# Softmax in 64-column chunks: the subtraction and the sum move from VectorE to ScalarE

## The chip, the cores and the metric

One core of a Trainium2 chip runs the whole program. The metric is the device time of one execution in microseconds (us), here 1665.19 us as the median of 3 runs before the change (1658.57 to 1665.71). Engines are named as in the profile: PE is TensorE (matmul) and PEld its weight load, DVE is VectorE, ACT is ScalarE, POOL is GpSimd, SP is SyncE, which only issues DMAs here.

## The reference

Attention within chunks of 64 tokens feeds two gated products. The change concerns the first function alone.

```python
def _attn_ref(q, k, v):                      # 8 batches, 8 heads, 576 tokens, 64 per head
    q_c, k_c, v_c = ...                      # 9 chunks of 64 tokens each
    scores = scale * np.matmul(q_c, k_c.transpose(0, 1, 2, 4, 3))
    scores = scores - np.max(scores, axis=-1, keepdims=True)
    attn = np.exp(scores)
    attn = attn / (np.sum(attn, axis=-1, keepdims=True) + 1e-09)
    out = np.matmul(attn, v_c)

x = _attn_ref(q, k, v)                       # as 4608 tokens x 512
x = (x @ w_a) * (x @ w_b) @ w_out            # inner width 1536
h = ((x @ w1) * (x @ w2)) @ w3               # inner width 1024
return h @ w_out2
```

## The kernel before, in words

The 4608 tokens are nine blocks of 512. A unit (class `Unit`) is one block and one pair of heads, so there are 36 units. Its scores are 16 products of 64x64: chunk n of the block goes to bank i = n mod 2 of two PSUM banks `s[0]` and `s[1]`, and the two heads stand on the upper and the lower 64 partitions. So each of the two banks holds four chunks of 64 columns (`chunks`, 256 of the bank's 512 columns), and the tile `e` in SBUF (128x512) holds all eight, sorted by `by_parity`.

The steps of a unit are: `load1`, `load2` (q, k, v by DMA), `turn` (q and k transposed: by VectorE, or in the first four blocks by TensorE with a copy by ScalarE out of two banks), `scores`, `soft1` (maximum per chunk and partition, subtraction, exponential), `soft2` (sum, plus 1e-9, reciprocal, multiplication), `flip` and `flip2` (`e` transposed into `pT`, by VectorE, or in the first four blocks by TensorE into a bank and a copy by ScalarE), `apply` (times v) and `put` (two copies of 128x256 out of PSUM, L410).

Nothing reorders the program at run time: each engine works through its own queue in the order in which the code emits, and waits there on semaphores. Four units stand alone in a prologue (the loop at L1174). The pieces of all others are emitted at the calls of `point()` between the products of the two gated layers. Blocks 0 and 1 are multiplied plainly (`plain_step`, L950); the later blocks go in pairs through a Strassen scheme with seven products per step (`strassen_step`, L895). Its order is P5, P1, P2, P6, P3, P7, P4 on the banks C, A, B, A, C, A, A: P6 and P4 add onto what P1 and P7 left in bank A, after ScalarE or VectorE has read the intermediate state (`held` is a copy c22, c11 or c12 by ScalarE, L914; `add` is VectorE's, L917). Behind P7 come the second layer's matmuls `acc` (L858) of the step before. L829 is the matmul line of all seven products and L815 that of the plain ones.

Units that run inside this loop use the PSUM banks that `state["banks"]` names: ("rB", "rD"). rB is also the bank of P2. Inside a burst of second-layer matmuls (`burst`, L985) they are acc2 and acc3. There is one buffer for each of the tiles `mx`, `sm`, `e` and `pT` outside of the prologue.

ScalarE also rounds every operand's high part (`split`, L242), converts weights (L180) and copies the plain products (L959). VectorE also forms low parts (L243), converts weights (L179 to L189) and multiplies.

Of the kernel before, what the change touches and what calls it, by code (L numbers as in the profile page):

```python
# [9 lines left out]
F32 = mybir.dt.float32  # L10
# [3 lines left out]
AF = mybir.ActivationFunctionType  # L14
ALU = mybir.AluOpType
AX = mybir.AxisListType

P = 128
NT = 512
CH = 64  # L20
# [58 lines left out]
def chunk_attention_two_gated_products(  # L79
# [23 lines left out]
    nc = tc.nc  # L103
# [8 lines left out]
    NCH = NT // CH  # L112
    HALF = NT // 2
    scale = 1.0 / float(D) ** 0.5
# [3 lines left out]
    pool = ctx.enter_context(tc.tile_pool(name="pool", bufs=1))  # L118
# [135 lines left out]
    class Unit:  # L254
# [93 lines left out]

        def soft1(self):
            mx = pool.tile([P, 2, NCH // 2], F32, tag="mx", name=f"mx{self.nm}")  # L350
            self.e = self.work("e")
            e4 = self.by_parity(self.e)
            for i in range(2):
                nc.vector.tensor_reduce(mx[:, i], self.chunks(self.s[i]), axis=AX.X, op=ALU.max)
            for i in range(2):
                nc.vector.tensor_tensor(
                    e4[:, i],
                    self.chunks(self.s[i]),
                    mx[:, i].unsqueeze(2).to_broadcast([P, NCH // 2, CH]),
                    op=ALU.subtract,  # L360
                )
            nc.scalar.activation(self.e, self.e, AF.Exp, scale=scale)

        def soft2(self):
            sm = pool.tile([P, NCH], F32, tag="sm", name=f"sm{self.nm}")
            e3 = self.e.rearrange("p (n k) -> p n k", k=CH)
            nc.vector.tensor_reduce(sm, e3, axis=AX.X, op=ALU.add)
            nc.vector.tensor_scalar_add(sm, sm, 1e-9)
            nc.vector.reciprocal(sm, sm)
            nc.vector.tensor_tensor(  # L370
                e3, e3, sm.unsqueeze(2).to_broadcast([P, NCH, CH]), op=ALU.mult
            )
# [720 lines left out]
    with tc.manual_schedule():  # L1093
# [241 lines left out]
        for ph, sb in [(0, sb) for sb in range(1, NSB + 1)] + [(1, sb) for sb in range(NSB + 1)]:  # L1335
# [39 lines left out]
            if lone:  # L1375
# [16 lines left out]
                class After:  # L1392
                    n = 0
# [71 lines left out]
```

## Time and profile before

| | |
|---|---|
| runs | 1665.71, 1665.19, 1658.57 us |
| profiled execution | span 1664.4 us from first to last instruction (the page gives no other time for it), mean granted TensorE clock 0.983 |
| PE busy | 1570.5 us, 94% |
| DVE busy | 899.0 us, 54% |
| ACT busy | 551.0 us, 33% |
| POOL busy | 571.5 us, 34% |
| chain that ended last | PE 73%, DVE 8%, DMA 5%, issue 4%, SP's queue 3%, ACT 3%, POOL 3% |

Busy times are sums over an engine's instructions. The chain is followed back from the last instruction, at each step to what released it. The busy share is an average over stages: attention lies in the first 880 us, where VectorE and ScalarE are fuller than behind. In a timeline an instruction stands with its start and duration in us; in brackets is the idle time of its engine before it and what ended that. In the granted clock, 1.00 is 2.4 GHz and 0.50 is 1.2 GHz.

### The profile page before, as it was taken

Reading aid. Unit: us, or ns where it says so; the run is one execution under the profiler, and the core shown is the slowest. Engines: PE = TensorE matmul, PEld = TensorE weight load, DVE = VectorE, ACT = ScalarE, POOL = GpSimd, SP = SyncE. Lnnn points to the kernel's source line nnn. Section 1 sums busy time; section 2 is a strip of 40 time slices with the busy share of each in tenths; the row PEclk is TensorE's granted clock in tenths of the full one; section 3 lists DMA queues with packets and bytes.
Section 4 is the critical chain, followed back from the end, with each engine's and each line's share of the span. In section 5 each row is a group of like instructions: output and inputs, shape, how many; then the busy total and the mean of one; then the engine's idle time right before and its main releaser. Section 6 shows DMA issues by size and latency. Waiting matters only on the chain.

```text
span 1664.4 us, 24572 instructions
## 1 busy us (share of the span) xinstructions
PE 1570.5 (94%) x8968; PEld 1256.9 (76%) x8968; DVE 899.0 (54%) x1460; ACT 551.0 (33%) x989; POOL 571.5 (34%) x578
## 2 busy tenths in 40 slices
PE   4789999899999999898999899999999999999998
PEld 3568777777776777676787677788878878878887
DVE  5768864786756555546776345554452352342331
ACT  4444534332342222332234222333332231331322
POOL 1435553322243211433446323323432332331432
PEclk9789999999999999999999999999999999999999
DMA  8668766887777777688997888886776666666684
GB/s 222 206 199 264 246 212 207 249 251 226 246 217 209 203 224 230 196 236 287 303 310 248 285 278 323 314 309 231 253 243 215 210 237 212 222 227 201 220 290 160
DMA packets 289976, 400.38 MB, mean 241 GB/s; under 512 B 175680, under 2 KB 196160, under 8 KB 289856
## 3 DMA queue, kind: packets, MB, share of 16 engines
q1 hardware_dynamic: 262688, 309.67, 60.9%
q0 software_dynamic: 23616, 81.80, 12.7%
q10 hardware_dynamic: 3552, 7.34, 1.2%
q8 instruction: 71, 1.16, 0.3%
q14 instruction: 49, 0.40, 0.1%
HBM read 312.74 MB, written 85.98 MB: 240 GB/s over the span
## 4 chain that ended last, share of the span: by engine, by line
PE 73%; DVE 8%; DMA 5%; issue 4%; SPq 3%; ACT 3%; POOL 3%; POOLq 0%; DVEq 0%; ACTq 0%
PE P L829 39%; PE acc L858 20%; PE wf L1082 3%; PE pb L815 3%; PE pa L815 3%; SPq L148 3%; DMA wo<-dwo 2%; PE pa0L L815 2%; PE pb0L L815 1%; PE x L396 1%; DVE c L917 1%; PE s L345 1%; ACT xP L242 1%; DMA d<-cv 1%; POOL cv L195 1%
## 5 line engine op out<-in xcount | busy, mean ns | idle before, releaser
L829 PE MATMUL P<-xP,w 128*128 128x512 f32 (+1 forms) x3102 | 715.5, 383 | 20.2 <-DVE c L917 16.5
L829 PEld LDWEIGHTS P<-xP,w 128*128 128x128 f32 x3102 | 557.0, 188 | 148.0 <-DVE c L917 23.3
L917 DVE TENSOR_TENSOR c<-P,c 128x512 f32<-128x512 f32 (+1 forms) x228 | 150.2, 661 | 302.5 <-PE P L829 301.8
L914 ACT COPY c<-P 128x512 f32<-128x512 f32 (+1 forms) x228 | 128.4, 563 | 222.9 <-PE P L829 222.3
L945 POOL TENSOR_TENSOR G<-c,c 128x512 f32<-128x512 f32 x68 | 88.6, 1304 | 311.1 <-DVE c L917 310.9
L242 ACT CAST gh<-c 128x512 fp32r<-128x512 f32 x68 | 42.3, 621 | 346.5 <-DVE c L944 346.5
L243 POOL TENSOR_TENSOR gl<-c,gh 128x512 fp32r<-128x512 f32 x68 | 90.3, 1328 | 162.3 <-ACT gh L242 158.7
L858 PE MATMUL acc<-gh,wo 128*128 128x512 f32 x384 | 138.8, 400 | 0.0
L944 DVE TENSOR_TENSOR c<-P,c 128x512 f32<-128x512 f32 x68 | 47.0, 691 | 137.7 <-PE P L829 137.7
L858 PE MATMUL acc<-wo,gh 128*128 128x512 f32 x320 | 111.2, 390 | 0.5 <-ACT gh L242 0.5
L858 PEld LDWEIGHTS acc<-gh,wo 128*128 128x128 f32 x384 | 72.8, 190 | 16.6
L195 POOL TENSOR_TENSOR cv<-cv 128x512 f32<-128x512 f32 x40 | 46.9, 1172 | 101.7 <-DVE cv L189 101.6
L243 DVE TENSOR_TENSOR xP<-xP,xP 128x512 fp32r<-128x512 f32 (+1 forms) x56 | 63.9, 1182 | 25.9 <-ACT xP L242 25.9
L815 PE MATMUL pa<-xq,w 128*128 128x512 f32 x288 | 76.0, 416 | 0.0
L858 PE MATMUL acc<-gl,wo 128*128 128x512 f32 x192 | 75.7, 394 | 0.0
L815 PE MATMUL pb<-xq,w 128*128 128x512 f32 x288 | 74.3, 409 | 0.0
L858 PEld LDWEIGHTS acc<-wo,gh 128*128 128x128 f32 x320 | 60.1, 188 | 13.9 <-ACT gh L242 1.0
L815 PEld LDWEIGHTS pa<-xq,w 128*128 128x128 f32 x288 | 57.1, 201 | 13.2
L867 ACT COPY ev<-acc 128x512 f32<-128x512 f32 x72 | 42.3, 587 | 71.0 <-PE acc L858 65.9
L815 PEld LDWEIGHTS pb<-xq,w 128*128 128x128 f32 x288 | 55.1, 196 | 11.6
L858 PE MATMUL acc<-wo,gl 128*128 128x512 f32 x160 | 63.0, 394 | 0.8 <-POOL gl L243 0.8
L157 POOL DMA_DIRECT2D dw<-w x58 | 32.4, 559 | 83.2 <-DVE w L243 80.3
(160 smaller groups left out, 2458.6 us busy)
## 6 DMA issues: line engine op xcount, KB each, us to landing
w<-dw SPq DMA_DIRECT2D x213, 512.0 KB, 4.4
wo<-dwo SPq DMA_DIRECT2D x168, 512.0 KB, 4.8
dw<-w POOLq DMA_DIRECT2D x58, 512.0 KB, 4.8
w<-dw SPq DMA_DIRECT2D x87, 256.0 KB, 3.3
d<-cv POOLq DMA_DIRECT2D x40, 256.0 KB, 5.2
su<-d SPq DMA_DIRECT2D x20, 512.0 KB, 4.9
cv_o<-in_moe_w_out_dram SPq DMA_DIRECT2D x18, 512.0 KB, 5.7
x2d<-ev POOLq DMA_DIRECT2D x36, 256.0 KB, 5.1
```

The source lines that it names most:

```text
L148: nc.sync.dma_start(*asks["left"].popleft())
L195: eng.tensor_tensor(self.w, hi.bitcast(F32), lo, op=ALU.add)
L242: nc.scalar.copy(dst_h, src)
L243: eng_l.tensor_tensor(dst_l, src, dst_h, op=ALU.subtract)
L815: nc.tensor.matmul(ps, w[m][:, kk // 2, wp, kk % 2], xq[kk // 2][:, kk % 2, xp], start=(n == 0), stop=(n == 3 * KM - 1),)
L829: nc.tensor.matmul(ps, w[:, wp, kt], x[:, kt, xp], start=(begins and n == 0), stop=(n == 5), skip_group_check=True,)
L858: nc.tensor.matmul(acc[m], a, b, start=(f == 0 and (wp, gp) == SEQ[0]), stop=(f == NF[ph] - 1 and (wp, gp) == SEQ[-1]),)
L914: nc.scalar.copy(t, src)
L917: add = lambda o, a, b: nc.vector.tensor_tensor(o, a, b, op=ALU.add)
L944: nc.vector.tensor_tensor(g, last, c11, op=ALU.mult)
L945: nc.gpsimd.tensor_tensor(g_place(ph, nm.split("_")[0], f, gplaces), c22, c12, op=ALU.mult)
L1082: nc.tensor.matmul(ps, t[:, gp, jj], wo2[jj // 2][:, jj % 2, wp], start=(jj == 0 and (wp, gp) == SEQ[0]), stop=(jj == NF[1] - 1 and (wp, g ...
```

## The change

The maxima are stored negated and multiplied by the scale in one more small VectorE instruction. VectorE's two subtractions and the single exponential over `e` are replaced by eight exponentials on ScalarE, one for each chunk of 64 columns, read straight out of the two score banks in alternation, each with the chunk's column of `mx` as its bias. Each of them also gives its chunk's sum into a column of `sm`, so the sum in `soft2` is gone. `sm` is now taken in `soft1`.

```diff
         def soft1(self):
             mx = pool.tile([P, 2, NCH // 2], F32, tag="mx", name=f"mx{self.nm}")
+            self.sm = pool.tile([P, NCH], F32, tag="sm", name=f"sm{self.nm}")
             self.e = self.work("e")
-            e4 = self.by_parity(self.e)
             for i in range(2):
-                nc.vector.tensor_reduce(mx[:, i], self.chunks(self.s[i]), axis=AX.X, op=ALU.max)
-            for i in range(2):
-                nc.vector.tensor_tensor(
-                    e4[:, i],
-                    self.chunks(self.s[i]),
-                    mx[:, i].unsqueeze(2).to_broadcast([P, NCH // 2, CH]),
-                    op=ALU.subtract,
+                nc.vector.tensor_reduce(
+                    mx[:, i], self.chunks(self.s[i]), axis=AX.X, op=ALU.max, negate=True
                 )
-            nc.scalar.activation(self.e, self.e, AF.Exp, scale=scale)
+            nc.vector.tensor_scalar_mul(mx, mx, scale)
+            for n in range(NCH):
+                m, i = divmod(n, 2)
+                nc.scalar.activation(
+                    self.e[:, n * CH : n * CH + CH],
+                    self.s[i][:, m * CH : m * CH + CH],
+                    AF.Exp,
+                    bias=mx[:, i, m : m + 1],
+                    scale=scale,
+                    accum_out=self.sm[:, n : n + 1],
+                )
 
         def soft2(self):
-            sm = pool.tile([P, NCH], F32, tag="sm", name=f"sm{self.nm}")
+            sm = self.sm
             e3 = self.e.rearrange("p (n k) -> p n k", k=CH)
-            nc.vector.tensor_reduce(sm, e3, axis=AX.X, op=ALU.add)
             nc.vector.tensor_scalar_add(sm, sm, 1e-9)
```

Lines behind the change stand four lines further down in the changed kernel (L829 becomes L833).

ScalarE's queue around the second unit of the third block pair, between P5 and P1. `c_1` are copies out of the products' banks (the first is c22, the second c11), `gh` and `w` are roundings, `s_4_1` are the two score banks of this unit. Before:

```order
L242 CAST gh_0_3543<-c_0_3455 128x512
L914 COPY c_1_3561<-P_1_3551 128x512
L362 ACTIVATE e_1_3586<-e_1_3586 128x512
L914 COPY c_1_3606<-P_1_3596 128x512
L242 CAST w_2_1_3621<-su_2_3433 128x2x256
L914 COPY c_1_3638<-P_1_3596 128x512
```

And now (the eight exponentials alternate between the two banks):

```order
L242 CAST gh_0_3628<-c_0_3540 128x512
L918 COPY c_1_3646<-P_1_3636 128x512
L360 ACTIVATE e_1_3672,sm_1_3671<-s_4_1_3652,mx_1_3670 128x64
L360 ACTIVATE e_1_3672,sm_1_3671<-s_4_1_3653,mx_1_3670 128x64
...
L918 COPY c_1_3698<-P_1_3688 128x512
L242 CAST w_2_1_3713<-su_2_3518 128x2x256
L918 COPY c_1_3728<-P_1_3688 128x512
```

What was one instruction out of SBUF between the copies of c22 and c11 is now eight out of PSUM, at the same place.

TensorE's queue at that place, with the semaphores that an instruction waits for (Activation is ScalarE's): the last scores, P1 and P2. Before:

```order
L345 MATMUL s_4_1_3568<-kT_1_3345,qT_1_3344 64x64 x2
L829 MATMUL P_1_3596<-xP_3110,w_1_0_3001 128x512 [waits DVE_49]
L829 MATMUL P_1_3596<-xP_3110,w_1_0_3001 128x512 x5
L829 MATMUL P_1_3608<-xP_3137,w_1_0_3001 128x512 [waits DVE_49,PE_49]
L829 MATMUL P_1_3608<-xP_3137,w_1_0_3001 128x512 x5
```

And now:

```order
L345 MATMUL s_4_1_3653<-kT_1_3432,qT_1_3431 64x64 x2
L833 MATMUL P_1_3688<-xP_3190,w_1_0_3081 128x512 [waits DVE_49]
L833 MATMUL P_1_3688<-xP_3190,w_1_0_3081 128x512 x5
L833 MATMUL P_1_3700<-xP_3217,w_1_0_3081 128x512 [waits DVE_49,Activation_49]
L833 MATMUL P_1_3700<-xP_3217,w_1_0_3081 128x512 x5
```

P2, the fourth and fifth row, now waits for ScalarE, since the last reader of the score bank in rB is an exponential.

VectorE's queue at the fourth unit of the third pair's second block, where `soft2` follows `soft1` at once; the last row is the addition that empties P7's bank. Before:

```order
L354 TENSOR_REDUCE mx_3_4966<-s_5_3_4948 128x4
L354 TENSOR_REDUCE mx_3_4966<-s_5_3_4949 128x4
L356 TENSOR_TENSOR e_3_4967<-s_5_3_4948,mx_3_4966 128x4x64
L356 TENSOR_TENSOR e_3_4967<-s_5_3_4949,mx_3_4966 128x4x64
L367 TENSOR_REDUCE sm_3_4973<-e_3_4967 128x8
L368 TENSOR_SCALAR sm_3_4973<-sm_3_4973 128x8
L369 RECIPROCAL sm_3_4973<-sm_3_4973 128x8
L370 TENSOR_TENSOR e_3_4967<-e_3_4967,sm_3_4973 128x512
L917 TENSOR_TENSOR c_10_4876<-P_10_4884,c_10_4876 128x512
```

And now:

```order
L354 TENSOR_REDUCE mx_3_5081<-s_5_3_5063 128x4
L354 TENSOR_REDUCE mx_3_5081<-s_5_3_5064 128x4
L357 TENSOR_SCALAR mx_3_5081<-mx_3_5081 128x8
L372 TENSOR_SCALAR sm_3_5082<-sm_3_5082 128x8
L373 RECIPROCAL sm_3_5082<-sm_3_5082 128x8
L374 TENSOR_TENSOR e_3_5083<-e_3_5083,sm_3_5082 128x512
L921 TENSOR_TENSOR c_10_4991<-P_10_4999,c_10_4991 128x512
```

Three long instructions are gone and a short one has come; L372 now is what waits for ScalarE, and the rest of the queue stands behind it as it stood behind L367.

## Rows read from the trace of the kernel before

**Rows 1.** The page's busy times: us, share of the span, instructions.
```profile
PE 1570.5 (94%) x8968; PEld 1256.9 (76%) x8968; DVE 899.0 (54%) x1460; ACT 551.0 (33%) x989; POOL 571.5 (34%) x578
```

**Rows 2.** Busy times in a stretch, by engine; last: clock, DMA share, GB/s.
```profile
42.00:200.00 158.00, 140.93 (x1096) 110.22 (x1095) 119.85 (x205) 73.19 (x123) 74.64 (x83) 0.92 0.73 228
```

**Rows 3.** Whom TensorE waited for, whole span: us in total, times, longest.
```profile
PE P L829 <- DVE c L917: 16.5, 15, 4.2
PE f L480 <- DVE e L370: 16.3, 9, 4.6
```

**Rows 4.** Instruction groups by form: busy us, mean ns, idle before and its releasers.
```profile
L914 ACT COPY c<-P 128x512 f32<-128x512 f32 x204 | 119.4, 586 | 210.3 <-PE P L829 209.9
...
L356 DVE TENSOR_TENSOR e<-s,mx 128x256 f32<-128x256 f32 x72 | 26.9, 415 | 0.0
...
L367 DVE TENSOR_REDUCE sm<-e 128x8 f32<-128x512 f32 x36 | 24.3, 674 | 3.8 <-ACT e L362 3.8
...
L362 ACT ACTIVATE e<-e 128x512 f32<-128x512 f32 x36 | 22.8, 633 | 96.3 <-DVE e L356 96.3
...
L410 ACT COPY x<-x 128x256 f32<-128x256 f32 x56 | 18.1, 376 | 24.5 <-PE x L396 24.1
```

**Rows 5.** Timeline of ScalarE, 326 to 329 us: start, duration, what, how many.
```profile
327.08 0.65 ACT L410 COPY x<-x 128x256 f32<-128x256 f32 x2 [2.41 <-PE x L396]
```

**Rows 6.** Timeline of one softmax after P3, 465 to 473 us.
```profile
465.83 0.74 DVE L354 TENSOR_REDUCE mx<-s 128x4 f32<-128x256 f32 x2
...
466.50 0.75 DVE L356 TENSOR_TENSOR e<-s,mx 128x256 f32<-128x256 f32 x2
...
467.34 0.63 ACT L362 ACTIVATE e<-e 128x512 f32<-128x512 f32 x1 [2.69 <-DVE e L356]
...
468.00 0.69 DVE L367 TENSOR_REDUCE sm<-e 128x8 f32<-128x512 f32 x1 [0.76 <-ACT e L362]
...
468.72 0.17 DVE L368 TENSOR_SCALAR sm<-sm 128x8 f32<-128x8 f32 x1
...
469.17 0.69 DVE L370 TENSOR_TENSOR e<-e,sm 128x512 f32<-128x512 f32 x1
...
470.51 1.66 PE L829 MATMUL P<-xP,w 128*128 128x512 f32 x6 [1.10 <-DVE c L917]
```

**Rows 7.** Timeline of one softmax between P5 and P1, 333 to 337 us.
```profile
333.01 1.66 PE L829 MATMUL P<-xP,w 128*128 128x512 f32 x6
334.18 0.74 DVE L354 TENSOR_REDUCE mx<-s 128x4 f32<-128x256 f32 x2
...
335.40 1.94 PE L829 MATMUL P<-xP,w 128*128 128x512 f32 x7 [0.72 <-DVE e L356]
```

**Rows 8.** Timeline of TensorE, 380 to 388 us: P4.
```profile
385.79 1.67 PE L829 MATMUL P<-xP,w 128*128 128x512 f32 x6 [1.77 <-DVE c L917]
```

**Rows 9.** Timeline of TensorE in the prologue: the fourth flip.
```profile
38.61 1.09 PE L480 MATMUL f<-ident,e 128*128 128x128 f32 x4 [4.56 <-DVE e L370]
```

**Rows 10.** Timeline of the first unit after the prologue, 50 to 58 us.
```profile
50.56 0.76 DVE L354 TENSOR_REDUCE mx<-s 128x4 f32<-128x256 f32 x2 [0.20 <-PE s L345]
...
52.61 1.04 ACT L468 COPY qT<-t 128x512 f32<-128x512 f32 x1
53.44 1.12 ACT L468 COPY kT<-t 128x512 f32<-128x512 f32 x1
...
54.73 0.90 PE L480 MATMUL f<-ident,e 128*128 128x128 f32 x4 [1.92 <-DVE e L370]
```

**Rows 11.** Timeline of TensorE, 118 to 126 us: a flip after a backlog.
```profile
123.64 0.63 PE L480 MATMUL f<-ident,e 128*128 128x128 f32 x4 [1.10 <-DVE e L370]
```

**Rows 12.** Timeline of TensorE, 224 to 236 us, after a wait for a DMA.
```profile
224.45 0.63 PE L467 MATMUL t<-ident,qk 128*128 128x128 f32 x4 [2.52 <-DMA qk<-in_k_dram]
224.83 4.58 PE L815 MATMUL pb<-xq,w 128*128 128x512 f32 x12
```

**Rows 13.** Busy times in the stretch behind it; the third number from the end is the clock.
```profile
225.00:230.00 5.00, 5.00 (x17) 3.92 (x16) 0.55 (x1) 1.52 (x2) 2.85 (x4) 0.66 0.39 117
```

## The prediction

> **What bounds the kernel now.** I read the page's table of busy times first, then the busy times by stretch, then who TensorE waited for, then the timelines around single softmaxes. TensorE is busy for 1570.5 of the 1664.4 us [rows 1], so the time changes only where an edit opens or closes a gap on TensorE. VectorE and ScalarE have idle time on average, and work taken from one or given to the other is by itself worth nothing. All 36 softmaxes lie in the first 880 us. There VectorE is crowded in one stretch, 119.85 of 158 us between 42 and 200 us [rows 2], and TensorE's two largest waits in the whole span are for VectorE: 16.5 us for the additions that empty a product's bank, and 16.3 us for the normalised `e` that the flip transposes [rows 3]. So softmax does stand on the path in places: this change is decided by how long one softmax takes from its scores to its `e`, by when it gives back its two PSUM banks, and by what is queued behind it on ScalarE.
>
> **What goes and what comes, per unit.** VectorE loses two subtractions of 415 ns and one sum of 674 ns [rows 4], and gains one small multiplication, priced below at 0.20 us: 1.3 us less per unit, 47 us in all. ScalarE loses one 633 ns exponential [rows 4] and gets eight of 128x64 out of PSUM, each with a bias read per partition and a sum to write out. No row shows that form. The nearest is the copy of 128x256 out of PSUM, 376 ns [rows 4]. Call E the time from the first of the eight to the end of the last.
>
> - Low end: the copies of 128x512 and 128x256 take 586 and 376 ns [rows 4], so 0.82 ns a column and 218 ns for 64 columns. Two of 128x256 in a row end 0.65 us after the first began [rows 5], so the second adds 0.27 us and a run overlaps by about 0.1. Eight then take 7 x 0.115 + 0.218 = 1.0 us, if bias and sum are free.
> - High end: each as long as the whole exponential of today, 633 ns: E = 5.1 us.
> - I take the nearest row unshortened, 376 ns each: E = 3.0 us. The smaller size pulls it down; the bias, and a sum that has to be delivered eight times, pull it up. Over 36 units ScalarE then gets 36 x (3.0 - 0.63) = 85 us more, which its average load would bear.
>
> **Break-even of a softmax.** In the unit at 465.83 us the maximum ends at 466.57, the exponential runs from 467.34, the sum starts at 468.00 and the normalisation ends at 469.86 [rows 6]. Afterwards: 466.57, plus 0.20 for the multiplication (the addition of the same size at 468.72 takes 0.17, and some 0.03 pass behind it), 0.09 to ScalarE (the subtraction ends at 467.25, today's exponential starts at 467.34), E, 0.03 back, and 1.14 for the small addition, the reciprocal and the normalisation (the 1.86 from sum to end, less the sum's own 0.72): 468.03 + E. The chain gets shorter only if E is under 1.83 us. With 3.0 it is 1.17 us longer.
>
> **Where that reaches TensorE.** Units whose softmax has slack (more than half of them) cost nothing: their flip comes several products later, and that work is the cover. The others, by place:
>
> 1. Five units after P5 (the second or third of a block pair, in L895's step): their scores stand between P5 and P1, and use the banks rB and rD. P2 writes into rB next and so must wait until the scores are read. Today the subtraction frees them: in the first, P1 starts at 333.01 and P2 at 335.40, 0.72 late [rows 7]. After the change the seventh of the eight exponentials frees that bank: maximum's end + 0.29 + 7/8 E. With 334.92 as that end, P2 starts at 337.84, 2.44 us later. The other four, with P1's 1.38 us as cover today, come out the same way at 2.74, 2.41, 2.41 and 2.40. Sum 12.4 us. The copy of c11, queued behind the eight on ScalarE, would end at about 338.8 and still hide beside P2, whose six matmuls take as long as P1's (1.66 us [rows 7]). VectorE's relief does not help here, since the bank's last reader has moved to ScalarE.
> 2. Two units after P3, where soft2 follows soft1 at once on VectorE and the addition that empties P7's bank stands behind it: P4 waits 1.10 us at 470.51 [rows 6]. The addition moves with the chain: 2 x 1.17 = 2.3 us. Two more of this kind have the transposes of q and k in between (P4's wait of 1.77 at 385.79 [rows 8]); there 2.7 us of E are covered, 0.3 each: 0.6 us.
> 3. The prologue: four units, each flip waiting for its `e`, the fourth for 4.56 us [rows 9], with ScalarE's casts for the weight conversion queued behind the exponentials and VectorE's conversion waiting for these casts. Three at the price of the tight chain; the fourth has slack, since VectorE converts in between, and gets half: 3.5 x 1.17 = 4.1 us.
> 4. Two units of the next block (the flips at 54.73 and 99.67): the maximum starts at 50.56, and the two copies of qT and kT, 1.95 us together, stand behind the exponential on ScalarE. The flip takes the bank that kT's copy empties, so it goes at 51.32 + 0.29 + E + 1.95 + 0.05 = 56.61 instead of 54.73 [rows 10]. 1.9 us each: 3.75 us.
> 5. Two units where VectorE comes to the sum late, out of a backlog, with the exponential long done: the flip's wait of 1.10 at 123.64 [rows 11] and its like at 188.78. Here the dropped sum is a gain, 0.7 us each: -1.4 us.
> 6. The clock. After a wait of 2.52 us at 224.45 the granted clock is 0.66 in 225 to 230 us, the level of 1.2 GHz for most of it, and twelve matmuls take 4.58 us [rows 12, 13]; after the wait of 1.77 at 385.79 six took 1.67, as many as at 333.01 behind no such wait [rows 7, 8]. Twelve at that pace would be 3.1 us, with the last one's tail of 0.2 counted once. The five waits of place 1 would be 2.4 to 3.2 us long, so each might cost another 1.5 us. The wait at 224.45 lay in a thinly filled stretch, these lie between full products; I take half: 3.8 us.
>
> Sum: 12.4 + 2.3 + 0.6 + 4.1 + 3.75 - 1.4 + 3.8 = 25.5 us on the span of 1664.4, so 1689.9. The page gives no other time for the profiled execution; its span is 0.8 us under the median of the runs (1665.2), which are themselves 7 us apart. Forecast: 1690 us.
>
> **Rivals.**
> - *The exponentials overlap.* If each of the eight adds what the second copy of the pair adds [rows 5], E = 0.376 + 7 x 0.27 = 2.27. Then place 1 is 9.2, place 2 is 0.9, the prologue 1.5, place 4 is 2.3, place 5 still -1.4, the clock nothing: 12.5, so 1678. For it: ScalarE's rows do overlap. Against it: each new one has a second operand and a second result. The Trainium skill (ScalarE: Activation LUTs, "What ACT_TABLE_LOAD costs") puts an ACTIVATE with a bias per partition at 280 ns plus 0.833 ns an element, 93 more than one without, with 93 of overlap in a run. The trace agrees on the slope (0.82). By that page E would be an estimated 2.0 and the time 1674 to 1675; it names no price for the sum.
> - *The sum is dear.* If delivering it makes each as long as today's exponential, E = 5.1: places 1 to 5 are 21.4, 6.5 + 4.7, 11.3, 7.9 and -1.4, the clock 7.5, in all 58: 1723. Nothing in the profile speaks for or against a dear sum, since no row has one.
> - *VectorE's backlog is what TensorE waits for* (the other side). With E at 1.0 the chain is 0.8 us shorter everywhere: the prologue gives back 2.8, place 2 gives 1.6 + 1.4, place 4 gives 0.2, place 5 gives 1.4, place 1 still costs 3.7; -3.7 in all, and if a third of the 16.5 us waited for additions [rows 3] goes with the relief, -9: 1656. It decides once E is under about 1.2 us. For it: the crowded stretch [rows 2]. Against it: only place 5 shows a backlog that a sum less would shorten, and an E of 1.0 needs bias and sum for nothing.
>
> **Chances and range.** Forecast (E of 2.6 to 3.6) 0.55, overlapping 0.25, dear sum 0.12, the other side 0.08. The forecast alone spans 1682 to 1703. The range goes below the overlapping case as far as 1669, where the shifts of places 3 and 4 (3.8 us) and half of place 1 (4.6 us) would vanish in later waits, and above the forecast into the dear one: 1669 to 1709. A change under 0.5% (8.3 us) cannot be told from none. Faster by more: half of the other side and a little, 0.05. Within: the rest of it and a third of the overlapping case, by that lower end of it: 0.12. Slower: 0.83.
>
> **What would show it.** Eight ACTIVATE rows per unit with a pitch of 0.37 us; ScalarE's busy time near 630 us and VectorE's near 850; P2 waiting for `e` on ScalarE five times at 2.4 to 3.2 us, with a clock under 1.0 right behind; P4's wait at 470 grown to 2.3 us; the first long product of the prologue some 4 us later. It is wrong if the eight end within 1.8 us, or if P2's wait stays under 1 us. Then places 1 to 4 fall together, since they hang on the same E.

## The result and the profile after

The changed kernel takes 1679.0 us (median of 4 runs, 1676.0 to 1680.1) against 1665.2 for the kernel before in the same session: ratio 1.0091, 95% interval 1.0074 to 1.0108, about 15 us slower by the ratio (13.8 by the two medians). The forecast was 1690 us, slower, with 1678 for the rival in which the exponentials overlap. The time landed beside that rival, but for another reason: two of my mistakes in the sum cancel, and a side effect of the change that I had not priced gives back some 7 us.

The busy times of the changed kernel, to be set beside [rows 1]:

```profile
PE 1570.9 (94%) x8968; PEld 1261.5 (75%) x8968; DVE 861.8 (51%) x1388; ACT 616.5 (37%) x1529; POOL 573.1 (34%) x578
```

VectorE lost 37 us of work (the prediction had 47), ScalarE got 66 more (85), TensorE is as busy as before; its span, 1678.3 us, is 13.9 longer, so in the sum the difference is gaps. The groups by form of the new softmax, in the columns of [rows 4]:

```profile
L360 ACT ACTIVATE e<-s,mx 128x64 f32<-128x64 f32 x288 | 86.0, 324 | 84.3 <-DVE mx L357 84.3
L360 ACT ACTIVATION_READ_ACCUMULATOR e<-s,mx 128x1 f32 x288 | 62.3, 216 | 0.0
L357 DVE TENSOR_SCALAR mx<-mx 128x8 f32<-128x8 f32 x36 | 9.2, 254 | 1.2
```

One exponential with a sum is two rows: an ACTIVATE and a read of the accumulator behind it, 288 of each. Whom TensorE waited for, in the columns of [rows 3]:

```profile
PE P L833 <- DVE c L921: 16.9, 15, 3.3
PE P L833 <- ACT e L360: 10.1, 5, 2.8
PE f L484 <- DVE e L374: 9.1, 4, 3.6
...
PE t L471 <- ACT e L360: 8.3, 5, 3.3
...
PE s L345 <- ACT e L360: 5.1, 3, 3.2
```

The waits for additions did not shrink (16.5 before [rows 3]): VectorE's relief buys nothing there. Flips wait 7 us less for VectorE's `e` than in [rows 3], but 3.6 us of that has only passed to waits for ScalarE (for the copies of kT, and for a weight's rounding). The 23.5 us of waits for ScalarE's `e` (10.1 + 8.3 + 5.1) are new. Each of those is a matmul that wants a PSUM bank which the exponentials have not read out yet.

The unit of [rows 7], between P5 and P1, in the timeline after:

```profile
342.07 0.74 DVE L354 TENSOR_REDUCE mx<-s 128x4 f32<-128x256 f32 x2
342.85 0.17 DVE L357 TENSOR_SCALAR mx<-mx 128x8 f32<-128x8 f32 x1
343.14 0.32 ACT L360 ACTIVATE e<-s,mx 128x64 f32<-128x64 f32 x1 [2.11 <-DVE mx L357]
343.35 0.19 ACT L360 ACTIVATION_READ_ACCUMULATOR e<-s,mx 128x1 f32 x1
343.44 0.30 ACT L360 ACTIVATE e<-s,mx 128x64 f32<-128x64 f32 x1
...
345.18 0.34 ACT L360 ACTIVATE e<-s,mx 128x64 f32<-128x64 f32 x1
345.37 0.96 PE L833 MATMUL P<-xP,w 128*128 128x512 f32 x3 [2.80 <-ACT e L360]
345.38 0.24 ACT L360 ACTIVATION_READ_ACCUMULATOR e<-s,mx 128x1 f32 x1
345.47 0.62 ACT L918 COPY c<-P 128x512 f32<-128x512 f32 x1
```

The eight start 0.29 us apart and are through 2.48 us after the first began (343.14 to 345.62): that is E. P2 starts when the seventh has been read, 2.80 us late where it was 0.72 late before [rows 7], and c11's copy starts on ScalarE behind the eighth. The clock behind that wait (third number from the end, as in [rows 13]), and behind the next of the five waits, of 2.12 us at 459.84, behind which it did not fall:

```profile
345.00:349.00 4.00, 3.63 (x11) 2.88 (x12) 1.73 (x5) 1.61 (x7) 0.10 (x1) 0.72 0.44 63
460.00:464.00 4.00, 4.00 (x18) 3.25 (x19) 2.27 (x5) 2.12 (x5) 0.60 (x1) 1.00 0.50 153
```
```profile
459.84 5.83 PE L833 MATMUL P<-xP,w 128*128 128x512 f32 x24 [2.12 <-ACT e L360]
```

Units of other kinds, in timelines after: P4 behind a softmax that stands after P3 (1.10 late in [rows 6]), and in the early blocks the scores of the second unit, the transposes of q and k, and the flip of [rows 10].

```profile
483.52 1.67 PE L833 MATMUL P<-xP,w 128*128 128x512 f32 x6 [1.79 <-DVE c L921]
```
```profile
18.30 1.02 PE L345 MATMUL s<-kT,qT 64*64 64x64 f32 x32 [3.17 <-ACT e L360]
...
57.59 1.97 PE L471 MATMUL t<-ident,qk 128*128 128x128 f32 x8 [3.35 <-ACT e L360]
...
60.76 1.11 PE L484 MATMUL f<-ident,e 128*128 128x128 f32 x4 [1.20 <-ACT kT L472]
```

The chain at 57.59 is one that the prediction did not have: the exponentials hold the bank that the next transposes of q and k write, the copies of qT and kT stand behind these transposes, and the flip behind the copies.

To see where the time goes I compare starts of the same instruction in two executions (24 first copies of a product on ScalarE, then 68 sums of products on GpSimd). TensorE's lag behind the profiled execution of the kernel before, in us, positive is later; the columns are times in that execution:

| kernel | 46 | 113 | 211 | 232 | 329 | 454 | 659 | 876 | 1554 |
|---|---|---|---|---|---|---|---|---|---|
| changed | +4.0 | +10.2 | +9.9 | +6.8 | +7.9 | +12.5 | +14.6 | +17.9 | +13.8 |
| only sm's request moved (e9) | +0.6 | -2.2 | -2.3 | -6.7 | -6.7 | -7.2 | -9.3 | -7.9 | -11.7 |
| first softmax old (e10) | +2.2 | +7.3 | +7.0 | +3.6 | +4.8 | +9.9 | +13.3 | +13.9 | +13.1 |
| new in slack units only (e3) | -0.1 | +0.6 | +0.4 | -3.1 | -1.9 | -2.4 | -3.4 | -0.8 | -0.8 |
| kernel before again (e12) | 0.0 | +3.4 | +3.4 | -0.9 | -0.9 | +0.7 | -0.7 | -1.1 | -0.6 |

Two things in the first row ask for a cause. The lag falls by 3.1 us between 211 and 232 us, and by 4.1 us behind 880 us, where no softmax runs any more. The experiments are about the size of E, about the places, and about these two.

### The profile page after: what moved, and what is told of

Its sections match the earlier page's. It is cut to its first block, busy times and chain, and to the rows that moved or that the text cites. A ratio compares the mean times of both kernels' runs of the same rounds, so it can differ in the third digit from the quotient of the medians.

```text
span 1678.3 us, 25053 instructions
## 1 busy us (share of the span) xinstructions
PE 1570.9 (94%) x8968; PEld 1261.5 (75%) x8968; DVE 861.8 (51%) x1388; ACT 616.5 (37%) x1529; POOL 573.1 (34%) x578
## 3 DMA queue, kind: packets, MB, share of 16 engines
q8 instruction: 71, 1.16, 0.3%
## 4 chain that ended last, share of the span: by engine, by line
PE 72%; DVE 8%; DMA 7%; ACT 5%; issue 4%; POOL 2%; SPq 2%; POOLq 0%; ACTq 0%; DVEq 0%
PE P L833 37%; PE acc L862 18%; PE pb L819 4%; PE pa L819 4%; PE wf L1086 3%; ACT e L360 2%; DMA wo<-dwo 2%; PE pa0L L819 2%; SPq L148 1%; PE x L400 1%; PE pb0L L819 1%; DVE c L921 1%; DVE xP L243 1%; DMA qk<-in_k_dram 1%; PE t L471 1%
## 5 line engine op out<-in xcount | busy, mean ns | idle before, releaser
L833 PE MATMUL P<-xP,w 128*128 128x512 f32 (+1 forms) x3102 | 714.5, 383 | 28.6 <-DVE c L921 16.9
L833 PEld LDWEIGHTS P<-xP,w 128*128 128x128 f32 x3102 | 559.7, 189 | 153.2 <-DVE c L921 23.8
L360 ACT ACTIVATE e<-s,mx 128x64 f32<-128x64 f32 x288 | 86.0, 324 | 84.3 <-DVE mx L357 84.3
```

Source lines behind the costliest of these rows:

```text
L360: nc.scalar.activation(self.e[:, n * CH : n * CH + CH], self.s[i][:, m * CH : m * CH + CH], AF.Exp, bias=mx[:, i, m : m + 1], scale=scale, ...
L833: nc.tensor.matmul(ps, w[:, wp, kt], x[:, kt, xp], start=(begins and n == 0), stop=(n == 5), skip_group_check=True,)
```

## Experiments

Each was timed against the kernel before on the same chip in the same session; e1 to e4, e5 to e8, e9 to e11 and e12 ran on four different chips, so across these groups ratios are compared, not medians. Intervals are 95%. The tile `sm` is asked for early, as in the changed kernel, in e1, e4 to e9 and e11, and late, as in the kernel before, in e2, e3 and e10; e9 shows what that is worth.

**e1: the five P5 units in the old form.** The softmax of before stands in the second branch.

```diff
...
+        def new(self):
+            return (self.j, self.hp) not in {(4, 1), (5, 2), (6, 1), (7, 2), (8, 1)}
+
+        def soft1(self):
+            (self.soft1_new if self.new() else self.soft1_old)()
```

> The softmax of before in the five units whose scores stand between P5 and P1, the new one in the other 31. Theory (the cost sits in a few places, and the largest is P2's wait for the score bank): the five waits of P2 for e on ScalarE, 10.1 us in the changed kernel, go back to 0.7, and the slow clock behind the first one (24 matmuls in 7.38 us where 5.89 were taken before) goes too: 9.4 + 1.5 = 10.9 us less than the changed kernel, so about 1668, 0.2 to 0.3% over before. Rival (ScalarE is simply fuller by 36 times the same price, and every unit adds its share): 5 of 36 shares of 14 us, 2 us less, about 1677.

Measured: 1668.1 us, ratio 1.0042 (1.0028 to 1.0055), half the loss gone: 8 us by the ratios. The lag at 876 us is +6.4 instead of +17.9: 11.5 us by the traces, for five softmaxes of 36. A softmax of place 1 costs about 2 us, and equal shares, which had 2 us for all five, are out.

**e2: the first eight softmaxes (blocks 0 and 1) old; e3: new only in the 21 units with slack.** The same branch with other sets:

```diff
# e2
+            return self.j > 1
# e3: also without the five units of e1 and two after P3
+            return self.j > 1 and (self.j, self.hp) not in {...}
```

> The softmax of before in the eight units of blocks 0 and 1, the new one in the other 28. Theory: these eight put TensorE 10.9 us behind at its 720th matmul, but the lag is 4.4 us at its 1620th, since later waits give way; so undoing them gains what is left, about 4.4 us: 1674. If the lag were not given back: 10.9 us, 1668. Rival (equal shares): 8 of 36 shares of 14 us, 3 us less, 1676.

> The new softmax only in the 21 units that stand neither in blocks 0 and 1, nor between P5 and P1, nor right behind P3 with soft2 at once. Theory: these have slack and cost nothing; VectorE's relief of 1.3 us each gives at most a little where it works off a backlog: 0.995 to 1.001 of before. Rival (equal shares): 21 of 36 of 14 us, 8 us more than before, 1.005.

Measured: e2 1676.5 us, ratio 1.0089 (1.0070 to 1.0107); e3 1662.9 us, 1.0000 (0.9987 to 1.0014). E3 shows that 21 softmaxes with slack together cost nothing beyond its interval of 2 us either way. E2 came out near the number expected, by a wrong reason: its lag up to 211 us is -0.8, so ten us of the changed kernel's early loss are away, and at 876 it is +9.2 against +17.9, so they are not given back later; yet the ratio is hardly better than the changed kernel's. E9 and e10 explain that: e2 asks for the sums' tile late, as the kernel before does, and lacks the gain that the changed kernel has by it.

**e4: the four chunks of one bank first, then those of the other**, so that the bank P2 wants is read after four exponentials, not seven.

```diff
-            for n in range(NCH):
-                m, i = divmod(n, 2)
+            for i in range(2):
+              for m in range(NCH // 2):
+                n = 2 * m + i
```

> The changed kernel with the eight exponentials in another order: the four chunks of the first score bank, then the four of the second. At a pitch of 0.293 us the bank in rB is free after four instead of seven, 0.88 us earlier. Theory (P2 waits for its bank): P2's five waits of 2.80, 2.12, 1.73, 1.75 and 1.73 fall by 0.88 each, 4.4 us, and the slow clock behind the first goes with it, 1.5: about 6 us less than the changed kernel, 1673. Rival (P2 waits because ScalarE's queue is late as a whole): no change, 1679.

Measured: 1675.9 us, ratio 1.0085 (1.0066 to 1.0103): 1 us under the changed kernel's 1.0091, where 6 were expected, and not distinguishable from no gain. TensorE's waits for `e` in the whole span, and the first two P2 in the timeline:

```profile
PE P L834 <- ACT e L361: 3.8, 4, 1.2
```
```profile
343.06 6.10 PE L834 MATMUL P<-xP,w 128*128 128x512 f32 x24 [1.91 <-DVE kT L334]
...
455.33 6.11 PE L834 MATMUL P<-xP,w 128*128 128x512 f32 x24 [1.22 <-ACT e L361]
```

At the bank the theory held: P2's five waits are 1.91 (now put down to VectorE), 1.22, 0.84, 0.86 and 0.84, 4.5 us less in all, and the clock does not fall behind the first. But the 24 matmuls behind the second take 6.11 instead of 5.83: P6 now waits for c11's copy, queued behind all eight. That gives back 0.3 us in each of four units and 0.9 in the fifth. Of the rest of the gain, part is lost at 830.36, where a product waits 1.69 us for a copy that stands behind a weight's conversion on ScalarE; for what is left no cause is shown, and the interval is wide enough to hold it.

**e5: the exponentials without the sum (VectorE adds as before).**

```diff
-                    accum_out=self.sm[:, n : n + 1],
...
+            nc.vector.tensor_reduce(sm, e3, axis=AX.X, op=ALU.add)
```

> The changed kernel, but the eight exponentials give no sums and VectorE sums e as before. In the changed kernel's trace each exponential is followed by an ACTIVATION_READ_ACCUMULATOR that starts 0.20 us behind it and holds the next one for 0.09. Without it the pitch should be 0.20 and E 1.75 instead of 2.47 us. Theory (bank and ScalarE's queue decide in the P5 units, the length of the chain elsewhere): P2's five waits are 0.63 shorter and the slow clock goes, 4.6 us less than the changed kernel; the chain to e is as long as with sums (0.72 less on ScalarE, 0.72 more on VectorE): 1.005 to 1.007 of before. Rival (the price is one of eight small instructions with a bias, the sums are free): as the changed kernel, 1.009.

Measured: 1671.3 us, ratio 1.0057 (1.0039 to 1.0075), as the theory had it. ScalarE's and TensorE's timeline and the clock in the stretch behind:

```profile
336.53 1.74 ACT L360 ACTIVATE e<-s,mx 128x64 f32<-128x64 f32 x8 [2.11 <-DVE mx L357]
```
```profile
338.12 7.17 PE L833 MATMUL P<-xP,w 128*128 128x512 f32 x23 [2.16 <-ACT e L360]
```
```profile
338.00:342.00 4.00, 3.88 (x12) 3.09 (x13) 1.99 (x4) 1.27 (x4) 0.33 (x1) 0.69 0.47 82
```

Eight in 1.74 us, a pitch of 0.20. The sum's read adds 0.09 to each, 0.74 of E's 2.48. P2's five waits are 6.9 us in all, 0.64 less each, as expected. The clock was expected not to fall, and it fell behind this wait of 2.16 as it did behind the 2.80.

**e6: VectorE's subtraction kept, eight exponentials from on-chip memory without a bias, with the sum.**

```diff
# against the kernel before
+            self.sm = pool.tile([P, NCH], F32, tag="sm", name=f"sm{self.nm}")
...
-            nc.scalar.activation(self.e, self.e, AF.Exp, scale=scale)
+            for n in range(NCH):
+                c = self.e[:, n * CH : n * CH + CH]
+                nc.scalar.activation(c, c, AF.Exp, scale=scale, accum_out=self.sm[:, n : n + 1])
...
-            nc.vector.tensor_reduce(sm, e3, axis=AX.X, op=ALU.add)
```

> VectorE keeps maximum and subtraction into SBUF as before; ScalarE takes eight exponentials in place there, without bias, that give the sums; VectorE's sum is gone. The score banks are given back by VectorE as before. Theory A (P5 units: the bank is the first thing in the way, ScalarE's queue the second): P2 waits 0.7 us once, but P6 now waits for c11's copy behind the eight, up to 1.9 us in each of the five; the tight chains are 0.4 us longer than in the changed kernel: 1.006 to 1.010. Theory B (only the bank matters there): the five units cost nothing: 1.002 to 1.004.

Measured: 1666.9 us, ratio 1.0031 (1.0015 to 1.0046). The group by form, and P2 and P6 of the same unit:

```profile
L365 ACT ACTIVATE e<-e 128x64 f32<-128x64 f32 x288 | 70.1, 245 | 85.1 <-DVE e L357 85.1
L365 ACT ACTIVATION_READ_ACCUMULATOR e<-e 128x1 f32 x288 | 53.9, 187 | 0.0
```
```profile
336.68 1.60 PE L831 MATMUL P<-xP,w 128*128 128x512 f32 x6 [0.72 <-DVE e L357]
...
339.20 4.45 PE L831 MATMUL P<-xP,w 128*128 128x512 f32 x18 [0.92 <-ACT c L916]
```

P2 is again 0.72 late, as before [rows 7]; the bank is free as soon as the subtraction has read it. P6 waits 0.92 for ScalarE's queue (0.85 to 1.34 in the other four), as theory A had it, but not up to 1.9, as the pitch is 0.24. The time lies in theory B's range, but e6 asks for `sm` early, which e9 below shows to be a gain of its own: against e9 it is 1.0031 - 0.9955 = 0.0076 slower, as theory A had it.

**e7: four of the eight exponentials done twice**, E about 3.64.

```diff
-            for n in range(NCH):
+            for n in [*range(NCH), *range(4)]:
```

> The changed kernel with four of the eight exponentials done a second time behind them, to the same values: E is 4 x 0.293 = 1.17 us longer, 3.64. Theory: P2's five waits are 1.17 longer (5.9 us), at 2.9 to 4.0 us long enough for the clock to fall behind each (one of five did, at 2.80): another 6; the four tight places 4 us; blocks 0 and 1 add little, since their lag is given back: 14 to 18 us over the changed kernel, 1.017 to 1.020. If the clock does not fall: about 1.014. Rival (ScalarE's load, every unit alike): 36 x 1.17 us x the 14 us that 36 x 1.84 us cost now, 9 us over the changed kernel.

Measured: 1713.1 us, ratio 1.0305 (1.0278 to 1.0332), 35 us over the changed kernel where 14 to 18 were expected. TensorE's waits:

```profile
PE t L471 <- ACT e L360: 17.8, 8, 5.2
PE P L833 <- ACT e L360: 17.1, 6, 4.0
PE s L345 <- ACT e L360: 8.6, 3, 4.3
```

With 1.16 us more per softmax the waits for `e` nearly double (43.5 us against 23.5) and reach more places (17 waits against 13). At 329 us TensorE's lag is already 18.8 us against 7.9, where the expectation had little for blocks 0 and 1, and at 876 it is 51.4 against 17.9. The price of E is not a line through the tight places: units with slack become tight. My count of places with a fixed cover each held for small changes of E alone. The clock fell behind four of the five P2, not behind each as expected; two of them, waits of nearly the same length:

```profile
580.77 7.41 PE L833 MATMUL P<-xP,w 128*128 128x512 f32 x24 [2.90 <-ACT e L360]
...
695.11 5.83 PE L833 MATMUL P<-xP,w 128*128 128x512 f32 x24 [2.92 <-ACT e L360]
```
```profile
580.00:584.00 4.00, 3.23 (x8) 2.56 (x9) 0.20 (x1) 1.49 (x9) 0.00 (x0) 0.60 0.82 246
695.00:699.00 4.00, 3.89 (x17) 3.19 (x18) 1.66 (x4) 1.41 (x5) 0.00 (x0) 1.00 0.29 109
```

**e8: no maximum at all** (it leaves the maximum out: two exponentials of 128x256 straight out of PSUM, VectorE adds), to see what the softmax would be worth if the chain got shorter.

```diff
# against the kernel before; the two tensor_reduce (ALU.max) and the two subtractions go
+            self.sm = pool.tile([P, NCH], F32, tag="sm", name=f"sm{self.nm}")
...
-            nc.scalar.activation(self.e, self.e, AF.Exp, scale=scale)
+                nc.scalar.activation(e4[:, i], self.chunks(self.s[i]), AF.Exp, scale=scale)
```

> Leaves out the maximum: ScalarE exponentiates each score bank in one instruction of 128x256 straight out of PSUM, without bias; VectorE sums as before. E is 0.65 us (the pair of copies of that size) and starts with the scores' end; VectorE is relieved of maximum and subtraction, 1.5 us per unit. Theory (TensorE waits for the end of the softmax chain and for its bank in few places): P2's wait is gone (-0.7), the tight places gain about 1.1 us each as far as they wait today, the flips of blocks 0 and 1 some 1 to 2 us each of which later waits take most: 0.993 to 0.998 of before. Rival (VectorE's load is what matters): 54 us of VectorE less, 36 of them in crowded stretches: 0.985 or lower.

Measured: 1645.3 us, ratio 0.9900 (0.9875 to 0.9926), between the two. It asks for `sm` early too, so its 16 us hold the 7.5 of e9 below; without them it lies in the theory's range. About 9 us are left for the shorter chain and the relief of VectorE, which this run does not separate.

**e9: the kernel before with one line moved; e10: the changed kernel with the first softmax old; e11: what might beat both.** Every kernel so far that gains 3 us or more behind 880 us asks for `sm` ahead of `e` in its first softmax, as the changed kernel does.

```diff
# e9, in soft1 of the kernel before; soft2 uses it
             mx = pool.tile([P, 2, NCH // 2], F32, tag="mx", ...)
+            self.sm = pool.tile([P, NCH], F32, tag="sm", ...)
             self.e = self.work("e")
# e10
+            return (self.j, self.hp) != (0, 0)
# e11, with the line of e9 in the old form too
+            return self.j in (2, 3)
```

> The kernel before, with one line moved: the small tile sm for the sums is asked for in soft1, ahead of e, instead of in soft2. No instruction is added, taken away or put in another order. What stays unexplained in the changed kernel is that from about 880 us on, where no softmax runs, it gains some 4 us on the kernel before, 0.09 us in each step of 12.4 us, with P4's six matmuls in 1.52 us instead of 1.56. It shows in every run so far in which the first softmax asks for sm ahead of e and in none of the others. Theory A (where the tiles lie in on-chip memory): the moved line alone gives it, about -4 us, 0.9975 (0.996 to 0.999), with six matmuls in 1.52 us behind 880 us and no difference up to there. Rival B (the lighter VectorE or the finer ScalarE work of the changed kernel gives it): nothing moves, 1.000 within 0.0015, six matmuls in 1.56 us.

> The changed kernel with the very first softmax (unit 0_0) alone in the old form, so that sm is first asked for in soft2 as in the kernel before; the other 35 are new. By A the gain behind 880 us goes: the lag of TensorE behind the kernel before stays constant from 880 us to the end. The first softmax's own cost in the prologue goes too (about 3 to 4 us), so that the time is near the changed kernel's (1.007 to 1.010 against the kernel before). By B the gain of 4 us behind 880 us stays and the time is 3 to 4 us under the changed kernel's, 1.005 to 1.007.

> What the other runs point to: the new softmax only in the eight units of blocks 2 and 3, where the run with it in 21 units gained 3.1 us by 232 us (the wait for the q and k load at 224.45 shrank), the old one in the 28 others, and sm asked for ahead of e. If both gains hold and add up: -3 and -4, 0.9955 (0.994 to 0.998). If the lag is taken back by the fixed waits behind block 3, as in that run (-1.9 at 329 us, -0.7 at the end): -0.7 and -4, 0.997. Without the gain of the early sm: 0.998 to 1.000.

Measured: e9 1654.6 us, ratio 0.9955 (0.9936 to 0.9973); e10 1682.0 us, 1.0120 (1.0100 to 1.0139); e11 1655.5 us, 0.9964 (0.9950 to 0.9977). E9 issues the same instructions in the same order as the kernel before and is 7.5 us faster. P4's six matmuls at 1300 to 1315 us of the kernel before, the changed kernel, e9 and e10, in that order:

```profile
1308.90 1.56 PE L829 MATMUL P<-xP,w 128*128 128x512 f32 x6
```
```profile
1312.01 1.52 PE L833 MATMUL P<-xP,w 128*128 128x512 f32 x6
```
```profile
1311.12 1.52 PE L830 MATMUL P<-xP,w 128*128 128x512 f32 x6
```
```profile
1309.54 1.56 PE L867 MATMUL P<-xP,w 128*128 128x512 f32 x6
```

The pace goes with the request for `sm`, in both directions, and not with the softmax: theory A holds, though e9's gain is about twice the 4 us expected, its lead up to 880 us was not expected at all, and e10, which loses it, is slower than the 1.007 to 1.010 expected. The tail gives 3.8 of it (the lag from 876 to 1554 us); the lead before that is 6.7 us by 232 us, of which the next experiment shows that a part is chance. In the compiled programs the moved line shifts three other buffers by 32 bytes in each partition: the first of `e`, the first of `w`, and one that holds `cv` early and xP4 later. In the tail of the kernel before, P4's products are the only ones of P1 to P7 whose streamed operand does not begin at a multiple of 64 bytes. P1 and P2 have in every second step a weight in that first buffer of `w`, which does not either. These are the products whose pace changes most: P1 in the kernel before with such a weight, P1 one step later with the other buffer, and P1 in e9:

```profile
1299.89 1.56 PE L829 MATMUL P<-xP,w 128*128 128x512 f32 x6
...
1312.37 1.52 PE L829 MATMUL P<-xP,w 128*128 128x512 f32 x6
```
```profile
1302.18 1.52 PE L830 MATMUL P<-xP,w 128*128 128x512 f32 x6
```

That placement is the cause is shown by e9. That it is this alignment was not tried on its own, and it is not the whole rule: P3 and P7 take 1.56 us in every one of these kernels though their operands begin at multiples of 64 bytes. Which of the three buffers gives the gain up front was not tried either.

E11 is no faster than e9: the new softmax in blocks 2 and 3 is worth nothing. The best version tried that keeps the maximum is the old softmax with `sm` asked for early.

**e12: the kernel before once more**, unchanged, for a second profiled execution.

> The kernel before once more, unchanged, for a second profiled execution of it. Every other kernel so far, the one with only a small tile moved among them, is 3.1 to 4.4 us earlier than the kernel before's profiled execution in one place, 211 to 232 us, where that execution waits 2.52 us for a load at 224.45 and then has 0.66 of the clock. Theory A (a mishap of that one execution, whose time is above the median of the kernel before's later runs): the second execution is itself 3 to 4 us earlier from 232 us on, without the 2.52 us wait, and even with the first one elsewhere; ratio 1.000 within 0.0015. Rival B (the wait belongs to the kernel before's placement and is cured by what moves tiles or lightens VectorE): the wait of about 2.5 us and the low clock are there again. Behind 880 us both expect the pace of the first execution, P4's six matmuls in 1.56 us.

Measured: 1659.3 us, ratio 0.9986 (0.9973 to 0.9999), which also says how far two sets of runs of one kernel can lie apart. In its trace no wait stands at 224 us; the loads of k are late elsewhere:

```profile
84.64 0.63 PE L467 MATMUL t<-ident,qk 128*128 128x128 f32 x4 [1.84 <-DMA qk<-in_k_dram]
...
100.88 1.09 PE L467 MATMUL t<-ident,qk 128*128 128x128 f32 x4 [3.14 <-DMA qk<-in_k_dram]
```

So the wait of 2.52 us [rows 12] and its slow clock [rows 13] belong to one execution. The fall of the lag by 3 to 4.5 us between 211 and 232 us, which all kernels in the table show, is this one accident of the execution they are compared with, no gain of theirs. Rival B is out. Of theory A the accident holds, but the second execution is only 0.9 us ahead at 232 us, not 3 to 4: behind its own late loads it was 3.4 us later at 113 us. A lag read in the first 235 us is good to 3 or 4 us only.

## Why the prediction was right in its direction and off in its sum

**What is compared.** With the three shifted buffers at the same places, the new softmax alone costs: changed kernel against e9, 1.0091 - 0.9955 = 0.0136, or 22.6 us, with the two intervals some 18 to 27 (the two profiled spans, 1678.3 and 1652.8, give 25.5); without e9, e10 against the kernel before, 20 us, and 1.8 more at 46 us for the first softmax that e10 leaves old. The forecast's sum was 25.5. The change also moved a tile, worth -7.5 us, which stood nowhere in the prediction. The measured 1679 is the one plus the other; its nearness to the rival's 1678 is no evidence for the rival's sum.

**E, on which everything hung.** Taken 3.0, measured 2.48: over the break-even of 1.83, so the sign was right, and between the forecast and the overlapping rival (2.27), under the 2.6 to 3.6 that I had given to the forecast. Neither of the two signs of being wrong came (the eight within 1.8 us, P2's wait under 1 us), but only one of P2's five waits lay in the 2.4 to 3.2 us that I had named. The term mis-sized is the nearest row taken unshortened: the pitch is 0.29, not 0.37. By e5, 0.20 of it is the exponential with its bias, and 0.09 the sum. The Trainium skill (ScalarE: Activation LUTs, "What ACT_TABLE_LOAD costs") gives 280 ns plus 0.833 an element for one with a bias, thus an estimated 333. The rows show 330 (e5) and 324: they agree. With the overlap of 93 ns that the same section gives, the pitch would be an estimated 0.24. That is longer than the 0.20 that e5 shows, so here the runs overlap by more. The sum, which that section does not price, made up the difference and a bit more.

**Place 1 (12.4 us).** The mechanism was right: P2 waits five times for ScalarE's `e`, 2.80, 2.12, 1.73, 1.75 and 1.73 us, 9.4 more than before. With E = 2.48 the prediction's own formula gives 10.1. E1 removes these five softmaxes and 11.5 us of lag with them.

**Place 6 (the clock, 3.8 us).** Once of five times: 24 matmuls took 7.38 us behind the wait of 2.80 and 5.83 behind the next, 1.5 us. The length of the wait does not decide it alone: in e5 the clock fell to 0.69 behind 2.16 us at the same place, in the changed kernel it stayed at full behind 2.12 at 459.84, and in e7 it fell behind 2.90 and stayed behind 2.92. Half the price for each of five was the wrong guess; one of five came to the full price.

**Place 2 (2.9 us).** P4's waits behind the two tight units grew from 1.10 to 1.79 and from 1.09 to 1.79, 0.7 each where 1.17 stood; with E = 2.48 it is 0.65. The two with transposes between got 0.2 shorter. Together +1.0.

**Places 3 and 4 (4.1 and 3.75 us).** These were too low, and here the step itself failed: I had the flips wait for `e`, and not the other user of the banks. The scores' banks are written again by the next scores (18.30, 3.17 late) and, in the next blocks, by the transposes of q and k (57.59, 3.35 late; 74.79, 2.35; 105.31, 1.60). Both wait for the last reader, and that reader is now ScalarE. I had seen this for place 1 and not asked it of the same two banks elsewhere. Nor had I priced the clock in these places. Against e9 the changed kernel is 3.4 us later at 46 us and 12.5 at 113, where places 3 to 5 came to 6.5 in the sum. The clock between 50 and 116 us (third number from the end), in the changed kernel and in e9:

```profile
50.00:116.00 66.00, 47.00 (x407) 34.86 (x406) 33.68 (x67) 34.53 (x104) 21.66 (x25) 0.77 0.63 191
```
```profile
50.00:116.00 66.00, 51.31 (x472) 38.95 (x471) 44.51 (x84) 30.27 (x50) 23.28 (x27) 0.87 0.67 206
```

TensorE's gaps from 46 to 113 us add up to 19.0 us in the changed kernel and 14.7 in e9, 4.3 more, and the lag grows by 9: the rest went with the slower clock. The kernel before has 0.82 and 0.77 in its two executions, so how much of the slow clock is the change's is not known. That and a load's wait of 3 to 4 us, which can lie in that stretch, bound what can be said of the waits' share. E2 and e10, which place tiles alike, differ by 0.0031, 5 us, for seven of the eight softmaxes, with intervals that overlap.

**Place 5 (-1.4 us).** Not seen: the flips at 133.63 and 198.66 still wait 1.18 and 1.11 us, where [rows 11] has 1.10; the first of them now waits for a rounding on ScalarE.

**Sum.** Behind 329 us the prediction had 12.4 + 2.9 + 3.8 = 19.1, and the changed kernel's lag against e9 grows by 11.2 there (from 14.6 to 25.8); up to 329 us it had 6.5, against 14.6. The rows behind 329 us account for that part (9.4 + 1.5 + 1.0 = 11.9). Errors of about -8 and +8 cancel, and that is luck: E was taken too long, and places 3 and 4 were taken too cheap. That the time itself came out 11 us under the forecast is mostly the moved tile. The other side (VectorE's backlog) fell: the waits for additions stayed at 16.9 us though VectorE does 37 us less. The dear sum fell too, since the read costs 0.09.

## What to carry to other kernels

In this kernel the last reader of a PSUM bank set when the next writer could start: when a cheap early reader (a subtraction) is replaced by a long late one, go through every later writer of that bank, not only the one where the wait shows today. Ask also what a new or moved allocation does to the addresses of the tiles around it, and run the kernel before with that move alone before a gain or loss of half a per cent is credited to the change (0.45% here). And profile the kernel before twice: a wait for a load that is in one trace and not in the other carries no argument.

## What the runs showed of the hardware that was not expected

- A sum taken along with an activation is an instruction of its own in the trace, 216 ns in its row; it overlaps the next ACTIVATE and adds 0.09 us to the pitch (0.20 without, 0.29 with, out of PSUM with a bias; 0.24 with it from on-chip memory without a bias).
- Moving buffers by thirty-two bytes changed P4's six matmuls from 1.56 to 1.52 us, and P1's where the weight's buffer had moved, and the kernel's time by 0.45% (0.27 to 0.64).
- A wait of 2.16 us lowered the granted clock to 0.69 in e5, and one of 2.12 us in the changed kernel did not lower it (1.00). In e7 one of 2.90 us lowered it to 0.60, and one of 2.92 us did not (1.00). The length of the wait alone does not decide.
